# The last product of a three-stage kernel turned round: weights stationary, tokens moving, and 32x32 block transposes ahead of the stores

## The chip, the core and the metric

The kernel runs on one core of one Trainium2 chip. The time is that of the device, in microseconds (us), for one launch. The core's engines are TensorE (PE; its weight loads are shown as PEld), VectorE (DVE), ScalarE (ACT), GpSimd (POOL) and SyncE (SP). Each works through its own queue in order, and semaphores order them against each other. In this kernel every DMA is issued from SP's queue.

## The reference

Three stages are chained. `attn` is a causal attention with a decay, over 4 batches of 8 heads with 576 positions; its output becomes x, 2304 tokens of 512 features. `moe` computes (((x w1) * (x w2)) w3) w_out. The kernel multiplies w3 by w_out first, and leaves the result, called z here, in DRAM. The change lies in the third stage alone:

```
h = x @ w_in                     # 2304 x 512 by 512 x 2048
P = a0 + a1*h + a2*h^2 + a3*h^3
Q = 1 + |b0|*|h| + |b1|*h^2
g = P / (Q + 1e-6)
out = g @ w_out                  # 2304 x 2048 by 2048 x 512
```

All of it is float32. The output is 2304 rows (tokens) of 512 floats, 2 KB a row.

## The kernel before, in words

**Products in three parts.** Every matmul operand is split in two float32r tiles, a high one and a low one (w and z have the suffix h or l, g is `gh` and `gl`). A product is three matmuls into the same PSUM bank: high by high, and the two mixed ones. `mm(po, A, B, start, stop)` loads A as weights (128 rows, up to 128 columns) and moves B past them; the result has A's columns on the partitions and B's columns along the row. All matmuls go through this helper, so they all have line 213.

**The last stage** goes over tokens in blocks of T2 = 512: four full ones and a last one of 256, NBLK2 = 5. In a block it goes over the 2048 inner features in 16 pieces of 128 (index fi), so that there are NI = 80 iterations, numbered i (L1004). One iteration i issues in this order:

- 12 matmuls for h of piece i (weights `wih`, `wil`; z's tokens move), into a bank given by `h_bank`: banks 6 and 7 in turn, after the first four.
- When the block before has just got its last piece, `out_block` (L956): eviction of the finished output banks into `o_sb` tiles and their stores.
- The out product of piece j = i - 3 (LAG = 3). Before the change, g's tokens are the weights, 128 tokens t at a time, and wo2's 512 features move. A full block has 4 tiles t, the last one has 2. Each tile holds one bank of 128 tokens x 512 features, over all 16 pieces.
- `rational(i)` (L972): ACT makes the square, the absolute value and the cubic's first step from h (L975 to L977), DVE makes the denominator (L982) and two Horner steps (L988, L989; L989 is the last reader of h's bank). ACT takes logarithm and exponential for the reciprocal (L986, L987), DVE finishes (L992, L995, L999). In the next iteration ACT rounds the result to `gh` (L967), and POOL makes `gl` (L968).

The out banks come from a ring of six (NO = 6, `out_bank`, L948). With four banks a block, two banks of a new block are free at once, and two are those of the block before, which `out_block` has to empty first. `out_block` empties even tiles on ACT (L962) and odd ones on DVE (L960), and issues one store per tile from SP (L964): 128 tokens, 256 KB, rows of 2 KB. There are 18 of each pair. After them in SP's queue stand the loads of the next z block (L892), issued at the start of a block.

Of the kernel before, what the change touches and what calls it, by code (L numbers as in the profile page):

```python
# [10 lines left out]
F32 = mybir.dt.float32  # L11
# [8 lines left out]
P = 128  # L20
# [153 lines left out]
def kernel(  # L174
# [16 lines left out]
    nc = tc.nc  # L191
    B, H, S, D = q.shape
    NT, DM = out.shape
# [5 lines left out]
    NF2 = DF2 // P  # L199
# [3 lines left out]
    T2 = 512  # L203
# [8 lines left out]
    def mm(o, lhsT, rhs, start, stop):  # L212
        nc.tensor.matmul(o, lhsT, rhs, start=start, stop=stop)  # L213

    def pool(name, side, **kw):
        return tc.tile_pool(name=name, bufs=1, side=side, reuse_waits="tile", **kw)
# [407 lines left out]
    for t in range(NCH * (NH + 1) + 2):  # L624
        n, c = divmod(t, NCH)
        p, x = n // 2, t % 2
# [128 lines left out]
    woh = wp.tile([P, NF1, DM], F32R, name="woh")  # L755
    wol = wp.tile([P, NF1, DM], F32R, name="wol")
# [69 lines left out]
    for i in range(NF1):  # L826
# [3 lines left out]
        po = ps_f[i % 2]  # L830
# [24 lines left out]
    woh = wl_.tile([P, NF2, DM], F32R, name="wo2h")  # L855
    wol = wl_.tile([P, NF2, DM], F32R, name="wo2l")
# [13 lines left out]
    bank = [psp.tile([P, 512], F32, name=f"bank{i}") for i in range(8)]  # L870
# [10 lines left out]
    def width(bi):  # L881
        return min(T2, NT - T2 * bi)
# [7 lines left out]
    def load_z(bi):  # L890
        for e in range(0, NKC, 2):
            nc.sync.dma_start(  # L892
                raw(zl[bi][:, e : e + 2]), z_dr[:, e : e + 2, T2 * bi : T2 * bi + width(bi)]
            )

    def split_z(bi, e):
        split(zh[bi][:, e], zl[bi][:, e])

    for i in range(NBLK):
        if 0 < i < NBLK - 1:  # L900
            load_c(i + 1)
        for e in range(NKC):
            g = NKC * i + e
            po = bank[g % 8][:, 0:T1]
# [27 lines left out]
    gp = ctx.enter_context(pool("gp", "left"))  # L932

    def ring(name, n, dt=F32):
        return [gp.tile([P, T2], dt, name=f"{name}{i}") for i in range(n)]

    h2, qv, rr, pp = ring("h2", 2), ring("qv", 2), ring("rr", 2), ring("pp", 3)
    gh, gl = ring("gh", 4, F32R), ring("gl", 4, F32R)
    NTK = T2 // P
    NO = 6  # L940
    o_sb = [gp.tile([P, DM], F32, name=f"o_sb{i}") for i in range(NTK)]
    NI = NBLK2 * NF2
    LAG = 3

    def at(r, i):
        return r[i % len(r)][:, 0 : width(i // NF2)]

    def out_bank(bi, t):  # L948
        return bank[(NTK * bi + t) % NO]

    def h_bank(i):

        b = (6, 7, 5, 4)[i] if i < 4 else 6 + i % 2
        return bank[b][:, 0 : width(i // NF2)]

    def out_block(bi):  # L956
        for t in range(width(bi) // P):
            o = o_sb[t]
            if t % 2:
                nc.vector.tensor_copy(o, out_bank(bi, t))  # L960
            else:
                nc.scalar.copy(o, out_bank(bi, t))  # L962
            r0 = T2 * bi + P * t
            nc.sync.dma_start(out[r0 : r0 + P, :], o)  # L964

    def g_split(j):
        nc.scalar.copy(at(gh, j), at(pp, j))  # L967
        nc.gpsimd.tensor_tensor(  # L968
            out=at(gl, j), in0=at(pp, j), in1=raw(at(gh, j)), op=ALU.subtract
        )  # L970

    def rational(i, h):  # L972


        nc.scalar.activation(at(h2, i), h, AF.Square)  # L975
        nc.scalar.activation(at(qv, i), h, AF.Abs, scale=pb_sb[:, 0:1])  # L976
        nc.scalar.activation(  # L977
            at(pp, i), h, AF.Identity, bias=pa_sb[:, 2:3], scale=pa_sb[:, 3:4]
        )
        if i > 0:  # L980
            g_split(i - 1)
        nc.vector.scalar_tensor_tensor(  # L982
            out=at(qv, i), in0=at(h2, i), scalar=pb_abs[:, 1:2], in1=at(qv, i),
            op0=ALU.mult, op1=ALU.add,
        )
        nc.scalar.activation(at(rr, i), at(qv, i), AF.Ln, bias=ln_bias, scale=2.0**-62)  # L986
        nc.scalar.activation(at(rr, i), at(rr, i), AF.Exp, bias=ex_bias, scale=-1.0)  # L987
        nc.vector.tensor_tensor(out=at(pp, i), in0=at(pp, i), in1=h, op=ALU.mult)  # L988
        nc.vector.scalar_tensor_tensor(  # L989
            out=at(pp, i), in0=at(pp, i), scalar=pa_sb[:, 1:2], in1=h, op0=ALU.add, op1=ALU.mult  # L990
        )
        nc.vector.scalar_tensor_tensor(  # L992
            out=at(qv, i), in0=at(qv, i), scalar=QC, in1=at(rr, i), op0=ALU.add, op1=ALU.mult
        )
        nc.vector.scalar_tensor_tensor(  # L995
            out=at(rr, i), in0=at(qv, i), scalar=2.0, in1=at(rr, i),
            op0=ALU.subtract, op1=ALU.mult, reverse0=True,
        )
        nc.vector.scalar_tensor_tensor(  # L999
            out=at(pp, i), in0=at(pp, i), scalar=pa_sb[:, 0:1], in1=at(rr, i),  # L1000
            op0=ALU.add, op1=ALU.mult,
        )

    for i in range(NI + LAG):  # L1004
        if i < NI:
            bi, fi = divmod(i, NF2)
            if fi == 0 and bi + 1 < NBLK2:
                load_z(bi + 1)
            hp_ = h_bank(i)
            fs = slice(P * fi, P * (fi + 1))  # L1010
            Z, L = zh[bi], zl[bi]
            for kc in range(NKC):
                mm(hp_, wih[:, kc, fs], Z[:, kc], kc == 0, False)
                mm(hp_, wih[:, kc, fs], L[:, kc], False, False)
                mm(hp_, wil[:, kc, fs], Z[:, kc], False, kc == NKC - 1)
        j = i - LAG - 1
        if 0 <= j and j % NF2 == NF2 - 1:
            out_block(j // NF2)
        j = i - LAG
        if j >= 0:  # L1020
            bo, fo = divmod(j, NF2)
            for t in range(width(bo) // P):
                po = out_bank(bo, t)
                tsl = slice(P * t, P * (t + 1))
                mm(po, at(gh, j)[:, tsl], woh[:, fo], fo == 0, False)
                mm(po, at(gh, j)[:, tsl], wol[:, fo], False, False)
                mm(po, at(gl, j)[:, tsl], woh[:, fo], False, fo == NF2 - 1)
        if i < NI:
            rational(i, hp_)
            if fi >= 8 and fi % 2 == 0 and bi + 1 < NBLK2:  # L1030
                split_z(bi + 1, (fi - 8) // 2)
        elif i == NI:
            g_split(NI - 1)
    out_block(NBLK2 - 1)


# [34 lines left out]
```

## Time and profile before

| what | value |
|---|---|
| time, median of 3 runs | 1007.89 us (1005.25 to 1012.77) |
| span of the profiled execution | 1007.3 us; no further time is listed for that execution |
| PE busy | 978.1 us, 97% of the span |
| DVE / ACT / POOL busy | 760.4 / 658.0 / 386.5 us |
| last stage | from about 603 us to the end |
| DMA | 114.94 MB in 125903 packets; under 512 B: 65521 |

Each is from the page of the profiled execution. The span runs from its first to its last instruction. Busy times of different engines overlap, so they don't add up to the span. A matmul's listed duration has its fill and drain, which overlap with those next to it; the rate of PE is read from the distance between starts.

### The profile page before, as it was taken

Reading aid. Unit: us, or ns where it says so; the run is one execution under the profiler, and the core shown is the slowest. Engines: PE = TensorE matmul, PEld = TensorE weight load, DVE = VectorE, ACT = ScalarE, POOL = GpSimd, SP = SyncE. Lnnn points to the kernel's source line nnn. Section 1 sums busy time; section 2 is a strip of 40 time slices with the busy share of each in tenths; the row PEclk is TensorE's granted clock in tenths of the full one; section 3 lists DMA queues with packets and bytes.
Section 4 is the critical chain, followed back from the end, with each engine's and each line's share of the span. In section 5 each row is a group of like instructions: output and inputs, shape, how many; then the busy total and the mean of one; then the engine's idle time right before and its main releaser. Section 6 shows DMA issues by size and latency. Waiting matters only on the chain.

```text
span 1007.3 us, 18126 instructions
## 1 busy us (share of the span) xinstructions
PE 978.1 (97%) x6032; PEld 859.5 (85%) x6032; DVE 760.4 (75%) x1690; ACT 658.0 (65%) x1443; POOL 386.5 (38%) x468
## 2 busy tenths in 40 slices
PE   6898999999999999999999999999999999999998
PEld 4676989999999999998899898888888888888886
DVE  5677886777777764979877729888788878877886
ACT  5677775766666663535555538767676767767686
POOL 7556772544444442644444302222222222222222
PEclk9999999999999999999999999999999999999999
DMA  5877664566666633664677651001001100100010
GB/s 130 216 179 199 187 141 116 145 186 182 175 175 183 165 103 111 199 211 160 201 246 242 211 159 37 1 14 70 1 1 42 43 1 8 37 20 1 1 43 21
DMA packets 125903, 114.94 MB, mean 114 GB/s; under 512 B 65521, under 2 KB 92145, under 8 KB 125809
## 3 DMA queue, kind: packets, MB, share of 16 engines
q1 hardware_dynamic: 125808, 113.79, 39.3%
q8 instruction: 47, 0.77, 0.3%
q14 instruction: 48, 0.39, 0.1%
HBM read 70.61 MB, written 23.22 MB: 93 GB/s over the span
## 4 chain that ended last, share of the span: by engine, by line
PE 79%; DVE 5%; DMA 3%; ACT 3%; issue 2%; SPq 1%; POOL 0%; ACTq 0%; DVEq 0%
PE bank L213 44%; PE ps_f L213 19%; PE ps_v L213 6%; PE ps_s L213 4%; PE ps_x L412 3%; PE ps_v L303 1%; DMA kh<-kh 1%; DMA wo2l<-wo_dr 1%; ACT rr L986 1%; DMA d_r<-in_moe_w_in_dram 1%; ACT rr L987 1%; DMA z_dr<-z_sb 1%; DVE pp L999 0%; DMA cl<-c_dr 0%; SPq L812 0%
## 5 line engine op out<-in xcount | busy, mean ns | idle before, releaser
L968 POOL TENSOR_TENSOR gl<-pp,gh 128x512 fp32r<-128x512 f32 (+1 forms) x80 | 95.3, 1191 | 318.5 <-ACT gh L967 312.0
L407 POOL TENSOR_SCALAR pr<-pr,st 128x128 f32<-128x128 f32 (+4 forms) x160 | 92.6, 590 | 145.2 <-DVE st L402 60.7
L381 DVE CUSTOM_DVE_ANT_0 pr<-ps_s,mask 128x128 f32<-128x128 f32 (+4 forms) x160 | 83.7, 523 | 71.4 <-PE ps_s L213 65.9
L213 PE MATMUL bank<-ch,wil 128*128 128x512 f32 (+1 forms) x320 | 118.3, 370 | 0.0
L213 PE MATMUL bank<-cl,wih 128*128 128x512 f32 (+1 forms) x320 | 118.2, 369 | 0.0
L213 PE MATMUL bank<-ch,wih 128*128 128x512 f32 (+1 forms) x320 | 117.8, 368 | 0.0
L213 PE MATMUL bank<-wo2h,gh 128*128 128x512 f32 x288 | 114.2, 397 | 0.8 <-ACT gh L967 0.8
L213 PE MATMUL bank<-wo2h,gl 128*128 128x512 f32 x288 | 114.1, 396 | 0.3
L213 PE MATMUL bank<-wo2l,gh 128*128 128x512 f32 x288 | 113.9, 396 | 0.0
L975 ACT ACTIVATE h<-bank 128x512 f32<-128x512 f32 (+1 forms) x80 | 44.3, 554 | 98.5 <-PE bank L213 98.4
L392 ACT ACTIVATE pr<-pr,st 128x128 f32<-128x128 f32 (+4 forms) x160 | 97.3, 608 | 12.7 <-DVE st L381 12.2
L982 DVE SCALAR_TENSOR_TENSOR qv<-h,pb_abs,qv 128x512 f32<-128x512 f32 (+1 forms) x80 | 55.8, 697 | 41.1 <-ACT qv L976 41.1
L436 ACT CAST pth<-ps_x 128x256 fp32r<-128x256 f32 (+1 forms) x96 | 44.5, 463 | 63.0 <-PE ps_x L412 43.5
L213 PE MATMUL bank<-cl,w3oh 128*128 128x256 f32 x288 | 81.4, 283 | 2.2 <-DVE cl L492 2.1
L213 PE MATMUL bank<-ch,w3oh 128*128 128x256 f32 x288 | 80.8, 280 | 1.1 <-ACT ch L491 1.0
L213 PE MATMUL bank<-ch,w3ol 128*128 128x256 f32 x288 | 80.6, 280 | 0.5 <-DVE w3ol L843 0.5
L412 PE MATMUL ps_x<-ident,pr 128*128 128x128 f32 (+1 forms) x480 | 74.7, 264 | 6.4 <-POOL pr L407 3.4
L213 PE MATMUL ps_s<-kh,qs 128*128 128x128 f32 (+2 forms) x192 | 75.6, 394 | 4.1 <-DMA kh<-kh 1.8
L992 DVE SCALAR_TENSOR_TENSOR qv<-qv,rr 128x512 f32<-128x512 f32 (+1 forms) x80 | 51.4, 643 | 28.5 <-ACT rr L987 28.5
L213 PEld LDWEIGHTS bank<-cl,wih 128*128 128x128 f32 x320 | 60.2, 188 | 11.7
L213 PEld LDWEIGHTS bank<-ch,wih 128*128 128x128 f32 x320 | 60.2, 188 | 11.7
L213 PEld LDWEIGHTS bank<-ch,wil 128*128 128x128 f32 x320 | 60.2, 188 | 10.3
(169 smaller groups left out, 3003.1 us busy)
## 6 DMA issues: line engine op xcount, KB each, us to landing
d_r<-in_moe_w_out_dram SPq DMA_DIRECT2D x48, 256.0 KB
c_dr<-c_sb SPq DMA_DIRECT2D x64, 144.0 KB
cl<-c_dr SPq DMA_DIRECT2D x36, 256.0 KB
d_r<-in_moe_w_dram SPq DMA_DIRECT2D x16, 512.0 KB
d_r<-in_moe_w_dram SPq DMA_DIRECT2D x32, 256.0 KB
d_r<-in_moe_w_in_dram SPq DMA_DIRECT2D x32, 256.0 KB
kh<-kh SPq DMA_DIRECT2D x45, 144.0 KB
z_dr<-z_sb SPq DMA_DIRECT2D x36, 128.0 KB
```

The costliest lines, as they stand in the source:

```text
L213: nc.tensor.matmul(o, lhsT, rhs, start=start, stop=stop)
L303: nc.tensor.transpose(ps[:, P * c : P * (c + 1)], flat(t[:, c]), ident)
L381: nc.vector.tensor_tensor_reduce(out=pr[0:r, OFF[c] + a : OFF[c] + b], in0=ps_s[(t + part) % 2][0:r, 0 : b - a], in1=mask[0:r, 512 - Q0[c] ...
L392: nc.scalar.activation(x, x, AF.Exp, bias=st[0:r, 0, c : c + 1], scale=-1.0, accum_out=st[0:r, 1, c : c + 1],)
L407: nc.gpsimd.tensor_scalar(x, x, st[0:r, 1, c : c + 1], 1.0, op0=ALU.mult, op1=ALU.mult)
L412: nc.tensor.transpose(ps_x[x][:, r * j : r * (j + 1)], pr[0:r, o + P * j : o + P * (j + 1)], ident[0:r, 0:r],)
L436: nc.scalar.copy(hi, src)
L968: nc.gpsimd.tensor_tensor(out=at(gl, j), in0=at(pp, j), in1=raw(at(gh, j)), op=ALU.subtract)
L975: nc.scalar.activation(at(h2, i), h, AF.Square)
L982: nc.vector.scalar_tensor_tensor(out=at(qv, i), in0=at(h2, i), scalar=pb_abs[:, 1:2], in1=at(qv, i), op0=ALU.mult, op1=ALU.add,)
L986: nc.scalar.activation(at(rr, i), at(qv, i), AF.Ln, bias=ln_bias, scale=2.0**-62)
L992: nc.vector.scalar_tensor_tensor(out=at(qv, i), in0=at(qv, i), scalar=QC, in1=at(rr, i), op0=ALU.add, op1=ALU.mult)
```

## The change

The out product is turned round. For each of NE = 4 groups e of 128 output features, a 128 x 128 block of `woh` or `wol` is the weights, and all of the block's tokens of `gh` or `gl` move (512 columns, in the last block 256). A bank then holds 128 features x 512 (or 256) tokens. The last block has 4 banks where it had 2, and 12 matmuls of 256 columns a piece where it had 6 of 512.

`out_block` empties all four banks on DVE, each with one `nc.vector.transpose`, which transposes every 32 x 32 block in place. Partition 32i + a then holds, for each n, token 32n + a and 32 features in a row. From each bank four DMAs go out, one for each 32 partitions; each takes 32 partitions x 16 (or 8) pieces of 32 floats, 128 B, to different rows of the output. A full block has 16 stores of 64 KB, the last block 16 of 32 KB. ACT has no part in it.

The text of the change defines `h_bank` and `out_block` twice; the second definitions are those that are called, and the first are left out here.

```
-    NTK = T2 // P
     NO = 6
-    o_sb = [gp.tile([P, DM], F32, name=f"o_sb{i}") for i in range(NTK)]
+    NE = DM // P
+    o_sb = [gp.tile([P, T2], F32, name=f"o_sb{i}") for i in range(NE)]
...
-    def out_bank(bi, t):
-        return bank[(NTK * bi + t) % NO]
+    def out_bank(bi, e):
+        return bank[(NE * bi + e) % NO][:, 0 : width(bi)]
...
     def out_block(bi):
-        for t in range(width(bi) // P):
-            o = o_sb[t]
-            if t % 2:
-                nc.vector.tensor_copy(o, out_bank(bi, t))
-            else:
-                nc.scalar.copy(o, out_bank(bi, t))
-            r0 = T2 * bi + P * t
-            nc.sync.dma_start(out[r0 : r0 + P, :], o)
+        w = width(bi)
+        rows = out[T2 * bi : T2 * bi + w].rearrange("(n a) d -> a n d", a=32)
+        for e in range(NE):
+            o = o_sb[e][:, 0:w]
+            nc.vector.transpose(o, out_bank(bi, e))
+            for i in range(P // 32):
+                d = P * e + 32 * i
+                nc.sync.dma_start(
+                    rows[:, :, d : d + 32],
+                    o[32 * i : 32 * (i + 1)].rearrange("p (n b) -> p n b", b=32),
+                )
...
             bo, fo = divmod(j, NF2)
-            for t in range(width(bo) // P):
-                po = out_bank(bo, t)
-                tsl = slice(P * t, P * (t + 1))
-                mm(po, at(gh, j)[:, tsl], woh[:, fo], fo == 0, False)
-                mm(po, at(gh, j)[:, tsl], wol[:, fo], False, False)
-                mm(po, at(gl, j)[:, tsl], woh[:, fo], False, fo == NF2 - 1)
+            for e in range(NE):
+                po = out_bank(bo, e)
+                mm(po, woh[:, fo, P * e : P * (e + 1)], at(gh, j), fo == 0, False)
+                mm(po, wol[:, fo, P * e : P * (e + 1)], at(gh, j), False, False)
+                mm(po, woh[:, fo, P * e : P * (e + 1)], at(gl, j), False, fo == NF2 - 1)
```

## Rows read from the trace of the kernel before

**Rows 1.** Page, part 1: engine, busy us (share of span), xinstructions.
```profile
PE 978.1 (97%) x6032; PEld 859.5 (85%) x6032; DVE 760.4 (75%) x1690; ACT 658.0 (65%) x1443; POOL 386.5 (38%) x468
```

**Rows 2.** Windows: stretch, length, busy us of PE, PEld, DVE, ACT, POOL; clock, DMA, GB/s.
```profile
700.00:800.00 100.00, 100.00 (x435) 81.33 (x434) 81.07 (x118) 70.04 (x115) 23.49 (x18) 1.00 0.09 32
```

**Rows 3.** Chain that ended last, from 900 us: start, us, what, xpieces merged.
```profile
899.93 67.83 PE bank L213 x328
...
969.39 0.51 ACT rr L986
...
972.31 0.51 ACT rr L986
...
999.50 2.17 issue
```

**Rows 4.** Timeline: matmul starts in a full block, then in the last block.
```profile
698.25 0.39 PE L213 MATMUL bank<-ch,wih 128*128 128x512 f32 x1
...
701.00 0.40 PE L213 MATMUL bank<-wo2h,gh 128*128 128x512 f32 x1
...
703.79 0.39 PE L213 MATMUL bank<-ch,wih 128*128 128x512 f32 x1
...
994.36 0.28 PE L213 MATMUL bank<-ch,wih 128*128 128x256 f32 x1
...
995.78 0.40 PE L213 MATMUL bank<-wo2h,gh 128*128 128x512 f32 x1
```

**Rows 5.** Timeline around the first block's eviction.
```profile
701.53 1.28 DVE L960 COPY o_sb<-bank 128x512 f32<-128x512 f32 x2
...
702.39 0.40 PE L213 MATMUL bank<-wo2h,gh 128*128 128x512 f32 x1
...
704.11 0.75 DVE L989 SCALAR_TENSOR_TENSOR pp<-pp,pa_sb,bank 128x512 f32<-128x512 f32 x1
...
709.34 0.39 PE L213 MATMUL bank<-ch,wih 128*128 128x512 f32 x1
```

**Rows 6.** Timeline of DVE, then ACT, around the fourth block's eviction.
```profile
961.73 1.28 DVE L960 COPY o_sb<-bank 128x512 f32<-128x512 f32 x2
962.92 0.48 DVE L982 SCALAR_TENSOR_TENSOR qv<-h,pb_abs,qv 128x256 f32<-128x256 f32 x1
963.38 0.42 DVE L988 TENSOR_TENSOR pp<-pp,bank 128x256 f32<-128x256 f32 x1
...
963.52 0.53 ACT L986 ACTIVATE rr<-qv,ln_bias 128x256 f32<-128x256 f32 x1
...
966.46 0.51 ACT L986 ACTIVATE rr<-qv,ln_bias 128x256 f32<-128x256 f32 x1
```

**Rows 7.** Line 594 and its like: a DVE scan; duration min/median/max, first and last start.
```profile
L594 DVE TENSOR_TENSOR_SCAN xr<-xr,xtmp x1: 1346/1346/1346, 4.8 to 4.8; 32x576 f32<-32x576 f32 x1
```

**Rows 8.** Timeline of the end.
```profile
1002.45 0.50 PE L213 MATMUL bank<-wo2h,gl 128*128 128x512 f32 x1
...
1002.98 0.59 ACT L962 COPY o_sb<-bank 128x512 f32<-128x512 f32 x1 [1.45 <-PE bank L213]
...
1003.60 1.14 SPq L964 DMA_DIRECT2D out_dram<-o_sb  x2
```

**Rows 9.** DMA issues by line: xcount, ns min/median/max on SP's queue, first and last start.
```profile
L964 SPq DMA_DIRECT2D out_dram<-o_sb x18: 332/351/412, 699.9 to 1004.4; - x18
L292 SPq DMA_DIRECT2D q_raw<-in_q_dram x16: 602/652/753, 2.2 to 323.2; - x16
L331 SPq DMA_DIRECT2D qb<-crow_dr x30: 223/252/987, 16.2 to 334.3; - x30
```

**Rows 10.** Windows with DMA (last two columns: share of 16 engines, GB/s): start, end.
```profile
2.00:5.00 3.00, 0.69 (x4) 0.71 (x4) 1.49 (x2) 0.69 (x2) 2.83 (x5) 1.00 0.67 158
...
1005.00:1006.00 1.00, 0.00 (x0) 0.00 (x0) 0.00 (x0) 0.00 (x0) 0.00 (x0) 1.00 0.81 311
1006.00:1007.00 1.00, 0.00 (x0) 0.00 (x0) 0.00 (x0) 0.00 (x0) 0.00 (x0) 0.54 0.00 0
```

More of the change, by code (lines that the diff above doesn't have):

```diff
@@ L956, in out_block, with h_bank @@
     def out_block(bi):
-        for t in range(width(bi) // P):
-            o = o_sb[t]
-            if t % 2:
-                nc.vector.tensor_copy(o, out_bank(bi, t))
-            else:
-                nc.scalar.copy(o, out_bank(bi, t))
-            r0 = T2 * bi + P * t
-            nc.sync.dma_start(out[r0 : r0 + P, :], o)
+        w = width(bi)
+        rows = out[T2 * bi : T2 * bi + w].rearrange("(n a) (c i b) -> c i a n b", a=32, c=NE, b=32)
+        for e in range(NE):
+            o = o_sb[e][:, 0:w]
+            nc.vector.transpose(o, out_bank(bi, e))
+            nc.sync.dma_start(rows[e], o.rearrange("p (n b) -> p n b", b=32))
+    def h_bank(i):
+        b = (6, 7, 5, 4)[i] if i < 4 else 6 + i % 2
+        return bank[b][:, 0 : width(i // NF2)]
+    def out_block(bi):
+        w = width(bi)
+        rows = out[T2 * bi : T2 * bi + w].rearrange("(n a) d -> a n d", a=32)
+        for e in range(NE):
+            o = o_sb[e][:, 0:w]
+            nc.vector.transpose(o, out_bank(bi, e))
+            for i in range(P // 32):
[4 more added lines that the diff above has]
+                )
     def g_split(j):
@@ L1021 @@
             bo, fo = divmod(j, NF2)
-            for t in range(width(bo) // P):
-                po = out_bank(bo, t)
-                tsl = slice(P * t, P * (t + 1))
-                mm(po, at(gh, j)[:, tsl], woh[:, fo], fo == 0, False)
-                mm(po, at(gh, j)[:, tsl], wol[:, fo], False, False)
-                mm(po, at(gl, j)[:, tsl], woh[:, fo], False, fo == NF2 - 1)
+            for e in range(NE):
+                po = out_bank(bo, e)
+                mm(po, woh[:, fo, P * e : P * (e + 1)], at(gh, j), fo == 0, False)
+                mm(po, wol[:, fo, P * e : P * (e + 1)], at(gh, j), False, False)
+                mm(po, woh[:, fo, P * e : P * (e + 1)], at(gl, j), False, fo == NF2 - 1)
         if i < NI:
```

## The prediction

> **What bounds the kernel now.** I read the page first, then stretches of 100 us, then the chain of waits, and last the timeline where the chain changes hands. PE is busy for 97% of the span [rows 1], and in a stretch of the last stage for all of it, with DVE at 81% and ACT at 70% [rows 2]. So for most of the stage only PE's columns count. But the chain ends elsewhere: PE holds it in one piece from 899.93 until 967.76, and from there it goes round ACT and DVE [rows 3]. In the last block PE has half the columns to do, while ACT and DVE don't halve. One turn from logarithm to logarithm takes 2.92 us (969.39 to 972.31), PE's own iteration 2.82 (below). From 968 to the end a delay of PE costs little and a delay of DVE or ACT is paid in full; after that comes a tail of eviction and stores.
>
> **PE's columns.** A full block has 12 out matmuls of 512 columns before and after. From 698.25 to 701.00 stand 12 h matmuls with w as weights and tokens moving, which is the form that the out product gets: 2.75 us. From 701.00 to 703.79 stand the 12 out matmuls of the old form: 2.79 us [rows 4]. I take no difference: the out product still changes its bank every third matmul, which h doesn't (the rivals come back to this). In the last block 12 matmuls of 256 replace 6 of 512; 12 h matmuls of 256 take 1.42 (994.36 to 995.78), six of 512 half of 2.79, 1.40 [rows 4]. That is 0.02 an iteration, on an engine which there has 0.1 to spare in each. So PE: 0, between -2.6 (64 full iterations by 0.04) and +0.3 (16 by 0.02).
>
> **Evictions inside the stage.** Before, DVE copies two banks, started 701.53, done after 1.28 [rows 5]; ACT copies the other two beside it. After, DVE does four. No transpose is in the trace. The nearest row is the copy itself (same engine, shape, PSUM source): 0.64. The bounds: below, the pitch of 0.60 at which two copies pass (961.73 to 962.92 [rows 6]), since 512 columns are still read; above, the slowest DVE row with one pass over a row, the scan with 1.346 us for 576 columns [rows 7], 1.2 us for 512. I take the copy.
>
> At the first block's end the third out group needs bank 0 at 702.39 and the fourth bank 1 three matmuls (0.70) later, 703.09. By the copy's time they are free at 701.53 + 0.64 + 0.05 = 702.2 and 702.9, in time. Behind the transposes in DVE's queue stands the next `rational`, whose last read of h (L989) was over at 704.86 and would be at 706.1; PE wants that bank at about 709.3 [rows 5]. There are 3 us of room, DVE has 19% idle to catch up [rows 2], and g has three iterations. Three such boundaries cost 0. ACT's two copies fall away, from an engine that isn't the bound there: 0.
>
> **The fourth eviction is different.** It comes at 961.73, in the short iterations. The two copies stand ahead of L982 (962.92), on which the logarithm at 963.52 waits; the next logarithm comes at 966.46, 2.94 later, so the turn of 2.92 is already closed [rows 6]. Two more DVE passes at a pitch of 0.60 push L982 to 964.1 and the turn by **1.2 us**, with no room behind it up to the last `gl`. (ACT loses its two copies, but then waits for L982.) Bounds: 0.9, if some 0.3 of slack is left, and 3.4 at the scan's rate (four by 1.2 less 1.28, less a little overlap).
>
> **The tail.** Before: the last `gl` releases a matmul at 1002.45 that takes 0.50; ACT's copy starts at 1002.98, the first store goes out at 1003.60, the second issue starts at 1004.4 [rows 8, 9], and the span ends at 1007.3, 2.9 later. After: that matmul starts at 1003.65 and is done after about 0.38 (half the columns, 0.12 less). The transpose of 256 columns goes at the price of L988, 0.42 from PSUM [rows 6]: first store at about 1004.5. The other three groups follow at 0.42 each, on DVE beside the stores. But SP now has **16 stores to issue, one after the other**, where it had two. The old store took 0.351 to issue. The new one has 32 partitions, its SBUF side runs on and its DRAM side is in pieces; the nearest row is L292, 64 partitions, 32 KB, in pieces of 256 B: 0.602 at least, 0.652 in the median. The cheapest DMA in the trace is L331 with 0.252, two partitions [rows 9]. I take 0.61, between L292's least and its median, bounds 0.25 and 0.75 (L292's longest).
>
> Fifteen issues by 0.61 are 9.15, so the last one starts at 1013.67. From there to the end it was 2.9; 0.84 of that moved 256 KB at 311 GB/s [rows 10], for 32 KB it is 0.3 (16 pieces an engine, priced below), while the issue is 0.27 longer: 2.6. The end is 1016.3, **+9.0 us**: 1.2 from the fourth eviction, 7.8 from the stores. With 0.25 the end is 1004.5 + 3.75 + 2.3 = 1010.6 (+3.3), with 0.75 it is 1018.5 (+11.2). The sum stands against the span of 1007.3; the median of the runs is 0.6 above it, so the time is 1007.9 + 9.0 = **1016.9**.
>
> Earlier blocks' stores (16 issues, about 10 us) are hidden: the next entry in SP's queue is a z load more than ten iterations of 5.5 us away, and the `o_sb` tiles are wanted again a block later. In that stretch DMA stands at 9% [rows 2].
>
> **Rival 1, the small pieces cost more than their issue.** The last block writes 4096 pieces of 128 B, 256 an engine. At the start, loads in 256 B pieces ran at 158 GB/s with the engines 0.67 busy: 617 pieces a us, 17 ns of an engine each [rows 10]. At that price the writes are 4.4 us, under the 9.8 of issue. No write under 512 B is in the rows. If each piece makes the engine fetch and write back what lies around it, as two passes of 512 B, the price is on the line through 17 ns for 256 B and 85 ns for a 2 KB row (311 GB/s at 0.81 [rows 10]): 27 ns for 512 B, 53 for two, 13.7 us in all. I let data start 1.0 us after the first issue begins (0.61 of it the issue); the end came 1.3 after the last data, which stopped at 1006 [rows 10]; so the end is 1004.5 + 1.0 + 13.7 + 1.3 = 1020.5, **+13.2**, 1021.1 on the runs. At worst a piece takes as long as a row: 21.8 us, +21. It decides from about 42 ns a piece (10.7 us of data); for it speaks that small pieces already run at half the rate of rows, against it that 17 ns is far below 42. Chance 0.22. The Trainium skill ("DMA: Bandwidth & Descriptors", Specifications) states this mechanism: below 512 B the DMA engine does a read-modify-write and misses line rate; no run here shows it so far.
>
> **Rival 2, slow transposes.** At 1.2 us each, bank 0 is free at 702.8 (0.4 late), bank 1 at 704.0 (another 0.45): 0.85 at each of three boundaries, 2.6 in all, and 2.2 more at the fourth. With the stores as above: +13.8, 1021.7. For it: the rows hold no transpose, and the scan shows that a DVE operation can take double; against it: L989, of the same width and also from PSUM, takes 0.75 [rows 5]. Chance 0.10.
>
> **Rival 3, not slower.** The 0.04 us by which the h form runs ahead of the old out form comes with the form, in 64 iterations: -2.6. Together with stores that issue as fast as L331 this gives +3.3 - 2.6 = +0.7; it is below zero once the form gains 0.055 or more an iteration. That gives 1004 to 1008.6. For it: the two forms differ in these rows, and weights no longer wait for `gh`. Against it: PE waits for nothing in this stretch, and a store like L331 has two partitions. Chance 0.08.
>
> **How the numbers follow.** The forecast, SP's issue as the tail, has the remaining 0.60, its own range +3.3 to +11.2, that is 1011.2 to 1019.1. A measurement of this kernel tells about 1%, 10.1 us, from no change. Above +10.1 lie a tenth or so of the forecast's chance (0.08), nearly all of rival 1 (0.20) and all of rival 2 (0.10): slower 0.38. Of rival 3 a part below -10 is hardly to be had; with the spread of runs I give faster 0.03. The rest, 0.59, is within 1%, with most of it on the slow side. The range 1010 to 1023 leaves out rival 3 (0.08) and rival 1's upper end (0.07).
>
> **What would show it.** In the changed trace: DVE's transposes near 0.64 for 512 columns; PE without idle at the first three boundaries; the logarithm after the fourth eviction about 1.2 later against its h; 16 issues back to back after the last matmul, with 0.6 each, and about 2.6 from the last one's start to the end. If the issues take 0.35, the tail is 4 us shorter and I am wrong on the largest term; if they end early and DMA engines stay busy after them, rival 1 holds; idle of PE at 702 rival 2; a step of the out matmuls under 0.229 rival 3.

## The result and the profile after

The changed kernel takes 1016.95 us, median of 7 runs (1014.36 to 1017.74); the one before took 1008.13 in the 7 runs beside them (1005.25 to 1012.77). The ratio is 1.0075, 95% interval 1.0053 to 1.0097, which is 5.3 to 9.8 us. The forecast was 1016.9, slower by less than 1%. The median fits to a tenth of a us, but that is in part luck: two terms made the forecast 2.5 us too long, and the scatter between runs nearly made up for it (below). The profiled run took 1016.98 us with a span of 1015.2.

The page of the changed kernel, parts 1 and 3. PE has 96 more matmuls than in [rows 1], and 38 thousand more packets under 512 B are moved (65521 before):

```profile
PE 978.6 (96%) x6128; PEld 865.6 (85%) x6128; DVE 766.2 (75%) x1701; ACT 654.2 (64%) x1434; POOL 385.1 (38%) x468
...
DMA packets 161455, 114.96 MB, mean 113 GB/s; under 512 B 103376, under 2 KB 130000, under 8 KB 161360
```

**Only the last stage may be compared.** Its first h matmul starts at 601.34 us in the kernel before and at 602.77 here, though the code up to there is the same. In the nine profiles of this study this start lies between 598.42 and 602.77, whatever was changed behind it. So 1.43 of the 7.9 us between the two spans are scatter of the earlier stages, and the change is read from the stage: 405.96 us before, 412.43 after, **+6.47**. In all nine the granted clock stays at 1.00, the higher of its two levels (2.4 GHz), from the stage's first matmul to its last, so the stages compare like with like. Below, times "in the stage" count from that first matmul. Three points of it, read from the timelines, divide the stage in every kernel (x1 to x7 are the experiments). The third is the first matmul of the very last piece that takes in `gl`; in every kernel but x7 it has waited for it. Spans are listed to 0.1 us, so the last column is good to 0.05:

| kernel | stage starts | logarithm after the fourth eviction | last piece's first gl matmul starts | from there to the end |
|---|---|---|---|---|
| before | 601.34 | 362.18 | 401.11 | 4.85 |
| after | 602.77 | 362.68 | 401.57 | 10.86 |
| x1, last block in the old form | 601.95 | 362.63 | 401.57 | 4.98 |
| x2, two issue queues at the end | 599.35 | 362.57 | 401.48 | 7.27 |
| x3, before with DVE evictions | 600.21 | 363.45 | 402.36 | 4.83 |
| x4, the turned form alone | 602.22 | 361.26 | 400.18 | 4.90 |
| x5, pieces of 1 KB at the end | 601.96 | 362.57 | 401.49 | 10.35 |
| x6, pieces of 64 B at the end | 598.42 | 362.67 | 401.59 | 11.59 |
| x7, three blocks turned, two old | 599.40 | 361.64 | 400.75 | 4.75 |

The first eviction of the changed kernel, in its timeline; what answers to [rows 5]:

```profile
702.76 2.50 DVE L974 STREAM_TRANSPOSE o_sb<-bank 128x512 f32<-128x512 f32 x4
703.52 0.19 PEld L213 LDWEIGHTS bank<-gh,wo2h 128*128 128x128 f32 x1 [0.19 <-DVE o_sb L974]
703.60 0.43 PE L213 MATMUL bank<-gh,wo2h 128*128 128x512 f32 x1
704.89 1.30 POOL L984 TENSOR_TENSOR gl<-pp,gh 128x512 fp32r<-128x512 f32 x1 [4.23 <-ACT gh L983]
705.19 1.55 DVE L998 SCALAR_TENSOR_TENSOR qv<-h,pb_abs,qv 128x512 f32<-128x512 f32 x1
706.77 0.72 ACT L1002 ACTIVATE rr<-qv,ln_bias 128x512 f32<-128x512 f32 x1 [2.01 <-DVE qv L998]
...
710.41 0.75 DVE L998 SCALAR_TENSOR_TENSOR qv<-h,pb_abs,qv 128x512 f32<-128x512 f32 x1
```

Four transposes pass in 2.50 us, 0.6 apart, as copies do. The weight load for the third group waits 0.19 us for bank 0, and the matmul behind it takes 0.43 where its like take 0.40. ACT waits 2.01 us for DVE; PE's next 15 iterations show no idle time. Part of ACT's wait isn't the transposes: L998, the denominator, takes 1.55 us where it takes 0.75 an iteration later. The four transposes push it into the 1.30 us in which GpSimd makes `gl`. This happens at each of the first three evictions (1.54 to 1.55 us each), and with DVE copies in x3 too (1.59); in the kernel before, the two never meet and the longest L982 (the same step) is near 0.75.

The fourth eviction, DVE and ACT; what answers to [rows 6]:

```profile
962.37 2.50 DVE L974 STREAM_TRANSPOSE o_sb<-bank 128x512 f32<-128x512 f32 x4
962.76 0.39 ACT L991 ACTIVATE h<-bank 128x256 f32<-128x256 f32 x1 [1.74 <-PE bank L213]
...
964.80 0.62 DVE L998 SCALAR_TENSOR_TENSOR qv<-h,pb_abs,qv 128x256 f32<-128x256 f32 x1
965.45 0.51 ACT L1002 ACTIVATE rr<-qv,ln_bias 128x256 f32<-128x256 f32 x1 [1.19 <-DVE qv L998]
...
968.37 0.51 ACT L1002 ACTIVATE rr<-qv,ln_bias 128x256 f32<-128x256 f32 x1
```

Here ACT's wait of 1.19 us for L998 (L982 before) is paid: the next logarithm is 2.92 behind, the closed turn of [rows 3]. But h came earlier: ACT takes it up 359.99 us into the stage, in the kernel before at 360.80. So the logarithm is only 0.50 later in the stage. L998 is again beside GpSimd's `gl` for a part of its time and takes 0.62, where a step of this width took 0.48 [rows 6].

The end, from the timeline; what answers to [rows 8]. Then the tile `o_sb` (columns as in [rows 9]) and windows of 1 us:

```profile
1004.34 0.38 PE L213 MATMUL bank<-gl,wo2h 128*128 128x256 f32 x1 [0.35 <-POOL gl L984]
...
1004.76 1.47 DVE L974 STREAM_TRANSPOSE o_sb<-bank 128x256 f32<-128x256 f32 x4 [1.77 <-PE bank L213]
...
1005.24 7.71 SPq L977 DMA_DIRECT2D out_dram<-o_sb  x16
```

```profile
L977 SPq DMA_DIRECT2D out_dram<-o_sb x80: 315/500/514, 703.5 to 1012.5; - x80
L974 DVE STREAM_TRANSPOSE o_sb<-bank x20: 415/672/709, 702.8 to 1005.8; 128x512 f32<-128x512 f32 x16, 128x256 f32<-128x256 f32 x4
```

```profile
1008.00:1009.00 1.00, 0.00 (x0) 0.00 (x0) 0.00 (x0) 0.00 (x0) 0.00 (x0) 1.00 0.41 66
...
1013.00:1014.00 1.00, 0.00 (x0) 0.00 (x0) 0.00 (x0) 0.00 (x0) 0.00 (x0) 0.50 0.39 63
1014.00:1015.20 1.20, 0.00 (x0) 0.00 (x0) 0.00 (x0) 0.00 (x0) 0.00 (x0) 0.50 0.00 0
```

DVE is done at 1006.2. From then on only SP and the DMA engines work: 16 issues in 7.71 us, the last at 1012.50, and 2.7 us more to the end. The DMA engines stand at 0.39 to 0.42 from 1006 to 1014. That is (0.41 x 16 engines) / (66 GB/s / 128 B = 516 pieces a us) = 12.7 ns of an engine per piece.

### The profile page after: what moved, and what is told of

The parts are those of the page before. It is cut to its first block, busy times and chain, and to the rows that moved or that the text cites. A ratio compares the mean times of both kernels' runs of the same rounds, so it can differ in the third digit from the quotient of the medians.

```text
span 1015.2 us, 18402 instructions
## 1 busy us (share of the span) xinstructions
PE 978.6 (96%) x6128; PEld 865.6 (85%) x6128; DVE 766.2 (75%) x1701; ACT 654.2 (64%) x1434; POOL 385.1 (38%) x468
## 4 chain that ended last, share of the span: by engine, by line
PE 78%; DVE 4%; ACT 3%; DMA 2%; issue 2%; SPq 1%; POOL 0%; DVEq 0%; ACTq 0%
PE bank L213 42%; PE ps_f L213 20%; PE ps_v L213 7%; PE ps_s L213 4%; PE ps_x L412 4%; PE ps_v L303 1%; DMA wo2l<-wo_dr 1%; ACT rr L1003 1%; ACT rr L1002 1%; DVE pp L1015 1%; DVE qv L1008 1%; DVE rr L1011 1%; DMA z_dr<-z_sb 1%; ACT gh L983 1%; DMA d_r<-in_moe_w_in_dram 0%
## 5 line engine op out<-in xcount | busy, mean ns | idle before, releaser
L213 PE MATMUL bank<-gh,wo2h 128*128 128x512 f32 (+1 forms) x320 | 119.4, 373 | 1.2 <-ACT gh L983 1.2
L213 PE MATMUL bank<-gl,wo2h 128*128 128x512 f32 (+1 forms) x320 | 118.5, 370 | 0.7 <-POOL gl L984 0.7
L213 PE MATMUL bank<-gh,wo2l 128*128 128x512 f32 (+1 forms) x320 | 117.8, 368 | 0.0
L392 ACT ACTIVATE pr<-pr,st 128x128 f32<-128x128 f32 (+4 forms) x160 | 97.2, 608 | 11.4 <-DVE st L381 10.7
L998 DVE SCALAR_TENSOR_TENSOR qv<-h,pb_abs,qv 128x512 f32<-128x512 f32 (+1 forms) x80 | 58.1, 727 | 36.2 <-ACT qv L992 36.2
L213 PEld LDWEIGHTS bank<-gl,wo2h 128*128 128x128 f32 x320 | 60.0, 188 | 12.6 <-POOL gl L984 1.1
L213 PEld LDWEIGHTS bank<-gh,wo2h 128*128 128x128 f32 x320 | 60.1, 188 | 12.5 <-ACT gh L983 1.6
```

The source lines that it names most:

```text
L392: nc.scalar.activation(x, x, AF.Exp, bias=st[0:r, 0, c : c + 1], scale=-1.0, accum_out=st[0:r, 1, c : c + 1],)
L998: nc.vector.scalar_tensor_tensor(out=at(qv, i), in0=at(h2, i), scalar=pb_abs[:, 1:2], in1=at(qv, i), op0=ALU.mult, op1=ALU.add,)
```

## The experiments

The theory: three things change, the turned form gains a little in the full blocks, the fourth eviction holds up the turn of ACT and DVE, and the end waits for SP's 16 issues. Its rivals: the time is lost inside the stage, or the small pieces hold up the DMA engines.

### x1: the last block alone in the old form

```
     def out_block(bi):
+        if width(bi) < T2:
+            ...                     # copies and stores as before the change
+            return
...
+            if width(bo) < T2:
+                ...                 # the three mm with gh, gl as weights
```

> The changed kernel, with the last block (256 tokens) alone back in the old form: g's tokens as weights, two banks, one ACT and one DVE copy, two stores of 128 rows of 2 KB. Theory (SP's 16 issues are the tail): the tail, from the last gl matmul's start to the end of the span, falls from 10.9 us back to 4.8 or 4.9, and the whole kernel stands at +0.5 against the kernel before (-0.8 from the turned form in the full blocks, +1.3 from the fourth eviction), 1008 to 1009 us beside 1008 before. Rival (the time is lost inside the stage, in the four evictions or in the form of the product): at least +4 against before remains. In the last stage, from the first h matmul to the last gl matmul's start, the theory expects 401.6 us as in the changed kernel, 401.1 in the one before.

Measured: 1009.85 us beside 1008.73, ratio 1.0008 (0.9984 to 1.0032). The timeline of its end:

```profile
1003.52 0.50 PE L213 MATMUL bank<-wo2h,gl 128*128 128x512 f32 x1
...
1004.66 1.16 SPq L978 DMA_DIRECT2D out_dram<-o_sb  x2
```

The last gl matmul starts at 401.57 in the stage, as in the changed kernel; the rest takes 4.98 in place of 10.86. So 5.9 of the 6.5 us lie in the last block: its form, its transposes or its stores. The remaining 0.6 is near the +0.5 that the theory has for the full blocks. That the form has no part in the 5.9 is shown by x4, which keeps it in the last block with four stores, and ends 4.90 us after the same point.

### x2: the last stores on two queues

```
+                q = nc.scalar if width(bi) < T2 and i % 2 else nc.sync
-                nc.sync.dma_start(
+                q.dma_start(
```

> The changed kernel; of the last block's 16 stores every second one is issued from ACT's queue, which has nothing else to do there. Same pieces, same bytes. Theory (issue on SP is the tail, 0.48 us each): eight issues a queue, so the time from the first issue to the end of the span falls by 8 x 0.48 = 3.8 us, from 10.0 to about 6.2, and the kernel stands at +3 to +5 against before where the changed one has +7 to +9. Rival (the 4096 pieces of 128 B hold up the DMA engines): no change, 10.0 us. In between, if at double the rate the engines become the limit: their share in the tail was 0.41 at 66 GB/s, so up to 2.4 times that rate has room.

Measured: 1012.10 us beside 1008.73, ratio 1.0026 (1.0008 to 1.0043). Timeline and one window of its end:

```profile
1001.73 3.83 SPq L978 DMA_DIRECT2D out_dram<-o_sb  x8
1001.73 3.95 ACTq L978 DMA_DIRECT2D out_dram<-o_sb  x8
```

```profile
1004.00:1005.00 1.00, 0.00 (x0) 0.00 (x0) 0.00 (x0) 0.00 (x0) 0.00 (x0) 0.79 0.84 131
```

From the first issue to the end of the span (1008.1) it is 6.4 us, in the changed kernel 10.0. Issue on one queue was the limit: on two queues the same pieces flow at 131 GB/s, double the rate, with the engines at 0.84, and a piece costs the same 13 ns (0.84 x 16 / 1023). Against the kernel before, the stage stands at +2.8, a little under the expected +3 to +5, since the changed one stands at +6.5 there and not at +7 to +9. By an estimate from the 0.84, a third queue could speed the pieces up by at most 1.2; it was not tried. Nor does a run tell what an issue's 0.4 to 0.45 us consist of.

### x3: the kernel before, with DVE doing all of a full block's copies

```
-            if t % 2:
+            if t % 2 or width(bi) == T2:
                 nc.vector.tensor_copy(o, out_bank(bi, t))
```

> The kernel before, with all four copies of a full block's eviction on DVE (before: two on ACT, two on DVE); the last block and all stores as before. It is the DVE part of the change alone, at the copy's price of 0.60 to 0.64 a bank. Theory: nothing at the first three evictions (PE without idle), and at the fourth the turn through ACT and DVE closes 1.2 to 1.3 us later and stays so: +1.2 to +1.3 us in all, with the last gl matmul's start at 402.3 to 402.4 us from the stage's first h matmul instead of 401.1. Rival (DVE has 19% idle and catches up in the last block too): 0, 401.1. Rival (PE stalls at the first evictions): more than +2.

Measured: 1009.89 us beside 1008.73, ratio 1.0012 (0.9993 to 1.0031), too coarse by itself. The stage shows it: 402.36. DVE and ACT at its fourth eviction:

```profile
960.56 2.48 DVE L960 COPY o_sb<-bank 128x512 f32<-128x512 f32 x4
962.95 0.67 DVE L982 SCALAR_TENSOR_TENSOR qv<-h,pb_abs,qv 128x256 f32<-128x256 f32 x1
```

```profile
963.66 0.51 ACT L986 ACTIVATE rr<-qv,ln_bias 128x256 f32<-128x256 f32 x1 [1.19 <-DVE qv L982]
...
966.59 0.51 ACT L986 ACTIVATE rr<-qv,ln_bias 128x256 f32<-128x256 f32 x1
```

The same 1.19 us of waiting as with transposes, the logarithm 1.27 later in the stage than before, and 1.25 us still there at the last piece's gl matmul, some 13 turns on. Not all of it is the two more copies: L982 itself takes 0.67 where it took 0.48 [rows 6], for it now runs beside GpSimd's `gl` for 0.39 of that. At the fourth block's last h, ahead of that eviction, the stage stands where it did (343.87 beside 343.91): the first three evictions cost nothing.

### x4: the turned form alone

```
-            nc.vector.transpose(o, out_bank(bi, e))
-            for i in range(P // 32):
-                ...
+            if e % 2:
+                nc.vector.tensor_copy(o, out_bank(bi, e))
+            else:
+                nc.scalar.copy(o, out_bank(bi, e))
+            r0 = T2 * bi + w // NE * e
+            rows = out[r0 : r0 + w // NE].rearrange("r (c d) -> (r c) d", d=w)
+            nc.sync.dma_start(rows, o)
```

> The turned product alone: matmuls as in the changed kernel, but banks emptied as before, by ACT and DVE copies in turn, and one store per bank, four a block, with rows of 2 KB (1 KB in the last block). The output's blocks are left untransposed. Theory: the form gains 0.8 us over the 64 full iterations (0.0127 each) and nothing else changes: last gl matmul's start at 400.3 us from the stage's first h matmul, the tail 4.6 to 5.2, the time 0.5 to 1.1 us under before. Rival 3 of the prediction at full size (0.04 us an iteration): -2.6, 398.5. Rival that the form changes nothing and 0.8 was scatter: 401.1.

Measured: 1009.33 us beside 1008.73, ratio 0.9994 (0.9976 to 1.0012): the medians and the ratio point different ways, and neither is clear of no change. In the stage the last gl matmul starts at 400.18, 0.93 earlier than before. Its end, four stores:

```profile
1002.40 0.38 PE L213 MATMUL bank<-gl,wo2h 128*128 128x256 f32 x1 [0.35 <-POOL gl L983]
...
1003.22 1.80 SPq L979 DMA_DIRECT2D out_dram<-o_sb  x4
```

The gain grows evenly. ACT takes up h of the last iteration of the first four blocks at 77.67, 166.41, 255.16 and 343.91 us in the kernel before, and at 77.50, 166.03, 254.57 and 343.10 here: 0.17, 0.38, 0.59, 0.81. The five other kernels with all full blocks turned show the same within 0.11 (343.10 to 343.21), and x3, with the old form, shows the old numbers. So it is no scatter. It is a third of what the prediction's rival 3 priced. The starts of a full iteration, out product, h, next out product, show where it lies; what answers to [rows 4]:

```profile
740.39 0.40 PE L213 MATMUL bank<-gh,wo2h 128*128 128x512 f32 x1
...
743.15 0.40 PE L213 MATMUL bank<-ch,wih 128*128 128x512 f32 x1
...
745.92 0.40 PE L213 MATMUL bank<-gh,wo2h 128*128 128x512 f32 x1
```

The out product's 12 matmuls take 2.76 us, those of h 2.77. In the median over the iterations of the first four blocks (20 to 340 us in the stage) the out product goes from 2.798 us to 2.763, and h, whose matmuls are the same in both kernels, from 2.748 to 2.770. The other five turned kernels have the same two medians, and x3 has those of the kernel before. So the turned product gains nearly all that rival 3 gave it (0.035 of 0.04), and h beside it loses 0.022; why h loses isn't shown.

### x5 and x6: larger and smaller pieces at the end

Both keep the 16 issues, their 32 partitions and their bytes; x5 sends pieces of 1 KB, x6 of 64 B.

```
+                if w < T2:
+                    r0 = T2 * bi + 16 * (4 * e + i)
+                    flat = out[r0 : r0 + 16].rearrange("r (c d) -> (r c) d", d=w)         # x5
+                    nc.sync.dma_start(flat, o[32 * i : 32 * (i + 1)])
...
+                    view = out[r0 : r0 + 16].rearrange("n (p b) -> p n b", b=16)         # x6
+                    nc.sync.dma_start(
+                        view, o[32 * i : 32 * (i + 1)].rearrange("p (n b) -> p n b", b=16)
+                    )
```

> The changed kernel; the last block's 16 stores are the same in number, partitions (32) and bytes (32 KB), but each partition's 256 floats go out as one piece of 1 KB: 512 pieces in place of 4096. They go to other places of the same block's rows, so the order of the output there is not the reference's. Theory A (an issue costs what its count of dimensions asks; an old store with rows took 0.35 us, the changed one 0.48): the distance of issues falls from 0.48 to 0.35 and the time from first issue to the end from 10.0 to about 7.9. Theory B (few partitions make an issue dear, pieces don't): 0.48 stays, 10.0. Rival (the pieces themselves hold up the end): the end comes nearer to the last issue, with 0.48 left, by more than 1 us.

> The changed kernel; the last block's 16 stores go out in pieces of 64 B, 8192 in place of 4096, with the same bytes, partitions and number of issues, to other places of the same block's rows (the order of the output there is not the reference's). Theory (issue on SP is the tail): the distance of issues stays at 0.48 and the end within 0.5 us of 10.0 after the first issue; the DMA engines' share in the tail, 0.41 before, rises towards 0.8, since a piece of 128 B took an engine 12.7 ns there and 64 B should take as long or little less. Rival (pieces are the price): the end moves by 3 us or more, towards 17 to 20 us after the first issue.

Measured, one run each: 1015.59 us (x5) and 1013.45 (x6), to be read from the stage alone. x5's issues and a window of its tail:

```profile
L980 SPq DMA_DIRECT2D out_dram<-o_sb x16: 325/419/421, 1004.3 to 1011.2; - x16
```

```profile
1009.00:1010.00 1.00, 0.00 (x0) 0.00 (x0) 0.00 (x0) 0.00 (x0) 0.00 (x0) 0.50 0.29 77
```

The same of x6:

```profile
L980 SPq DMA_DIRECT2D out_dram<-o_sb x16: 316/488/491, 1000.9 to 1008.7; - x16
```

```profile
1003.00:1004.00 1.00, 0.00 (x0) 0.00 (x0) 0.00 (x0) 0.00 (x0) 0.00 (x0) 1.00 0.57 60
```

From the first issue to the end it is 9.5 us with 512 pieces, 10.0 with 4096 and 10.7 with 8192. Theory A of x5 is refuted, B comes near: one dimension less and an eighth of the pieces take the distance of issues only from 0.48 to 0.46 (6.9 us over 15). The end comes 2.6 us after the last issue's start, before 2.7, so its rival falls too. Doubling the pieces adds 0.7 us, not 3; it moved a little more than the 0.5 that was expected, since the distance went to 0.52. The engines' share rose to about 0.6 and not towards 0.8. A piece of 64 B takes an engine 0.57 x 16 / (60000 / 64) = 9.7 ns. So the number of issues on a queue sets the end, and the shape of the pieces moves it by 0.5 to 0.7 us.

### x7: a mixed kernel

```
     def out_block(bi):
+        if bi >= 3:
+            ...                     # copies and stores as before the change
...
+            if bo >= 3:
+                n = width(bo) // P
+                steps = [(t, s) for t in range(n) for s in range(3)]
+                if j == NI - 1:
+                    steps = [(t, s) for t in range(n) for s in range(2)] + [(t, 2) for t in range(n)]
...
+            else:                   # turned, as in the change
```

> A mixed kernel: the first three blocks turned, with the four transposes and 16 stores a block; the fourth and the last block in the old form with its copies and stores. Also, in the very last piece, the two products with gh of both token tiles come ahead of the two with gl. Theory: three quarters of the form's gain (48 iterations by 0.0127, 0.6 us) and none of its two losses: the last gl matmul's start, 401.1 us from the stage's first h matmul in the kernel before, comes at 400.5; the new order of the last piece lets two matmuls run while gl is awaited, so the tail is 0.4 to 0.5 shorter than 4.85. Together -1.0 us against before, 1007 beside 1008, less than the times can tell apart but plain in the stage. Rival (the transposes and small stores of the first three blocks cost something somewhere in the stage): 401.1 or more.

Measured: 1010.02 us beside 1009.64, ratio 1.0007 (0.9991 to 1.0024): no difference in the time. The stage takes 405.5 us, 0.4 less than before, where -1.0 was expected. Its end, timeline and window:

```profile
1000.15 0.63 PE L213 MATMUL bank<-wo2h,gl 128*128 128x512 f32 x2
1000.58 0.58 ACT L976 COPY o_sb<-bank 128x512 f32<-128x512 f32 x1 [1.52 <-PE bank L213]
1000.82 0.69 DVE L974 COPY o_sb<-bank 128x512 f32<-128x512 f32 x1 [2.20 <-PE bank L213]
1001.19 0.81 SPq L978 DMA_DIRECT2D out_dram<-o_sb  x2
```

```profile
1002.00:1003.00 1.00, 0.00 (x0) 0.00 (x0) 0.00 (x0) 0.00 (x0) 0.00 (x0) 1.00 0.96 371
```

The form's part came as expected: the logarithm at 361.64, 0.54 earlier. Of the new order nothing is left. The gl matmuls no longer wait for `gl` (POOL was done at 999.93, 400.53 in the stage, as expected), and DVE's copy is over 1.6 us after gl, before it was 2.0. But the two stores of 256 KB now follow each other closely, with the DMA engines at 0.96 and 371 GB/s: the last row is out 1.92 us after the second issue's start, before it was 1.67, which takes back some 0.25 of the 0.4. The rest lies between the last row and the end of the span, and its cause is open. Of the kernels that leave the output in the reference's order this one has the shortest stage, by less than any time can tell; x4, which doesn't, is at 405.1.

## Why the prediction was right

**Right, with its mechanism.** The tail was to be SP's issues, one after the other, with DVE, PE and DMA engines under it; x1 and x2 show that. Of its steps the first store came 0.90 us after the last piece's first gl matmul (forecast 0.85, 1003.65 to 1004.5), and the end 2.7 after the last issue's start (2.6). The fourth eviction was to cost 1.2 us, with no room behind it: 1.27 and 1.25 in x3, with ACT's wait of 1.19 in both kernels. A part of that is a term which the prediction doesn't have: L982 beside GpSimd took 0.19 more in x3. The transposes were to go at the copy's price, and they do: median 0.672, 0.6 apart. The 0.64 of the forecast was half of a row in which two copies overlap; one copy took 0.68. The first three evictions were to cost nothing. Over three blocks x2 and x5, with the same transposes and stores, stand within 0.01 us of x4, and the changed kernel 0.11 behind it, which is the spread of equal kernels there. But the room was smaller than forecast: L998 beside GpSimd took 0.8 longer, so the last read of h (L1005) ended at 708.12, 5.36 after the first transpose began, where the prediction had 4.6 (701.53 to 706.1). The 3 us of room took that in.

**Mis-sized: the issue.** "I take 0.61, between L292's least and its median": it is 0.48 (7.71 / 16). That is 15 x 0.13 = 1.9 us too much, and the tail gained 6.0, not 7.8. L292 was near in shape, but the three shapes of x5, x6 and the changed kernel differ by only 0.06 in their distance. The old stores' own row, 0.332 to 0.412 [rows 9], would have been the better guide: see the last section.

**Mis-sized: the form.** "I take no difference" between the two forms of the out product: it gains 0.8 us by the fourth block's end, inside the bound of -2.6 but not 0. The prediction's argument was that the out product changes its bank every third matmul in either form; the out product gained 0.035 us an iteration all the same, and h lost 0.022. What in the operands' roles does this, no run here tells.

**The balance.** In the stage the sum should have been -0.8 + 1.3 + 6.0 = 6.5, where 9.0 was written. That is what the two profiles show (+6.47). The difference of medians, 8.8, is larger than that by 2.3. The ratio of 1.0075 is 7.6 us, and its interval takes in 6.5 and 8.8; in the profiled pair, 1.43 of the 7.9 between the spans came from stages that are the same. So the forecast of 1016.9 was nearer than its own terms deserve.

**The rivals.** Rival 1 fell: it needed 42 ns a piece, and a piece takes 13. The Trainium skill ("DMA: Bandwidth & Descriptors", Specifications) says that below 512 B the engine does a read-modify-write and that line rate needs 512 B or more. The second agrees with the rows, 128 B in 12.7 ns of an engine beside 2 KB in 85 ns, 10 and 24 GB/s. The first no run shows; if it happens here, it costs no more time of an engine than this, for a piece of 128 B takes less than the 17 ns of a 256 B load [rows 10]. Rival 2 fell with the 0.672 of a transpose. Rival 3 had a real cause, of which a third was left beside h's loss, and it needed stores that issue twice as fast.

## What to carry to other kernels

Where a kernel ends with stores, count the DMA issues behind the last result and multiply by the distance of back-to-back issues on one queue. The size of the pieces came second here, and a second, idle queue halved the issues' time (7.71 to 3.95 us). Work moved onto an engine is free as long as another engine is the limit, and costs all of it where the last, shorter block has turned the limit round: look at the stage's last part before taking an average of idle time. Look also at what a delayed step will then run beside: here it met another engine's work and took twice its time. Where two kernels share their first part, compare stages from their first instruction: here the spans scatter by 4 us ahead of the change, and the stage repeats to a tenth.

## What the runs showed of the hardware

**An issue alone is cheaper than one in a row.** The first of the 16 stores took 0.32 us on SP's queue, those behind it 0.39 to 0.45, and 0.48 from start to start; SP's timeline at 1005.24, and the 16 by line:

```profile
1005.24 0.32 SPq L977 DMA_DIRECT2D out_dram<-o_sb  x1
```

```profile
L977 SPq DMA_DIRECT2D out_dram<-o_sb x16: 315/448/450, 1005.2 to 1012.5; - x16
```

The issues of L292, 0.602 at least [rows 9], also stand in a row, each some 0.1 us or less behind the end of the one before it. What made them longer still was not tried.

**DVE beside GpSimd.** L998, which reads two tiles from SBUF, took 1.55 us in place of 0.75 where GpSimd's `gl` ran beside it for 1.00 of that, and 0.62 in place of 0.48 with 0.33 beside it; x3 shows the same without transposes (1.59 and 0.67). The step that reads h from its bank, L1005, ran wholly beside `gl` in most iterations and kept its 0.75. GpSimd's spans are rough, and in every case L998 also came right behind four evictions, which no run separates; but the loss goes with the time beside `gl` (0.80 for 1.00 us, 0.14 for 0.33).

Pieces of 64, 128 and 2048 B took a DMA engine 9.7, 12.7 and 85 ns, the last from [rows 10]. A DVE transpose of 32 x 32 blocks, f32 from PSUM, 128 x 512, took 0.672 us in the median; four in a row passed in 2.50 us, four copies of the same banks in 2.48 (x3). The product with w as weights and tokens moving took 0.035 us less per 12 matmuls and the h product beside it 0.022 more, in six kernels, 0.0127 a full iteration over the four blocks; the cause stays open.
